# A linear-attention block beside a mixture of experts: which expert is worked first, and the column width of its plain products

## The chip, the cores and the metric

The kernel runs on one core of a Trainium2 chip. The metric is the device time of one execution in microseconds, lower is better. The engines are named as in the profile: PE (TensorE: matrix products; PEld is its load of the stationary operand), DVE (VectorE), ACT (ScalarE), POOL (GpSimd), SP (the queue from which most transfers are issued). The core has 128 partitions; PSUM, into which PE writes, has 8 banks of 512 floats per partition.

## The reference

Input is 2048 tokens of 512 numbers. The output is the input, plus a linear attention over the layer-normed tokens, plus a mixture of eight experts of which each token takes its best two:

```python
xn = layernorm(x)                                  # (2048, 512)
q, k, v = split(xn @ wqkv)                         # 32 heads of 16
phi = lambda t: where(t > 0, t + 1, exp(t)) + 1e-6
kv, z = sum_s phi(k) v^T, sum_s phi(k)             # per head
attn = (phi(q) kv) / (phi(q) z + 1e-6) @ wo
top2 = argsort(-(xn @ w_gate))[:, :2]; gates = softmax over the two logits
for e in range(8):
    h = silu(xn @ w1[e]) @ w2[e]                   # 512 -> 1792 -> 512
    out += (gates of tokens that chose e) * h
return x + attn + out
```

## The kernel before

**Precision.** Each float32 matrix is split into a high and a low part (`split_hi` on ACT, `split_lo` on DVE, lines 141 and 144), and each product is three matmuls: high x high, high x low, low x high (`PASSES`).

**Stages.** Layer norm, the key projection and the routing come first. Then a loop over token tiles computes the queries, `q_proj` (line 1376), and output products, `o_proj` (line 1437); the routing's small DVE steps run beside it. The experts fill the rest, from about 194 us on. The last output products end the program.

**Experts.** The routing ranks the eight experts by how many tokens chose them, and place r of the order works the expert of rank r with room for `CAP[r]` tokens: 576, 552, 544, 528, 520, 512, 504, 496. The tokens of an expert are gathered in blocks of 128 (`gather1`, issued on POOL). The first expert's blocks are turned by PE transposes (`x_block`, line 1093) and copied out of PSUM by ACT (line 1096). The later experts' blocks go through DRAM: `x_out` (SP, line 1109) writes 32-row groups, `x_in` (SP, line 1117) reads them back, `x_turn` (DVE, line 1126) transposes 32 x 32 blocks.

**Pairs.** An expert's 1792 hidden columns are worked as 7 pairs of 128-column tiles, so there are 56 pairs, g = 0 to 55. A pair (r, j) computes its hidden tiles, and between those products PE works pieces of the second product `mm2` of the pair before: lines 1198 and 1201. A piece is three matmuls. For an expert of at most 512 places (`single`) there are 8 pieces a pair, all 512 columns wide. A larger one has 12: two blocks of 128 tokens with 512 columns each, and four with the tokens over 256 as columns; their results are turned on DVE (`y_turn`) and added to the output in 128-column rows (`y_put`), with gate values passed round by `gate_out`, `gate_in` and `gate_up`. Three pieces of each pair are held over to the front of the next.

**Two kinds of pair.** From the third pair on, `pair_fast` computes a pair by seven products of half the tokens (`PRODUCTS`), on sums and differences of token halves and weight quarters: 7 x 2 x 3 = 42 matmuls of `CAP[r] / 2` columns (line 1316). Its results are built up in two PSUM tiles, px and pz; the tile px gets product 0, 2, 4 and then 6, and between product 4 and product 6 a DVE add (line 1343) reads it. The first two pairs (`NPLAIN`) are `pair_plain`: no sums are needed, so they can begin early; 2 hidden tiles x 2 token halves x 4 row blocks x 3 passes = 48 matmuls of 288 columns (line 1294).

**What sets the order.** Each engine runs its instructions in the order of the program, and the jobs between the products are placed by tables: `plan` puts weight splits, `x_hi`/`x_lo` (splits of the token halves B11, B12, B21, B22 and of their differences T1 to T4) and the steps of the next expert (`FIRST`, `MOVES`, `YMOVES`) behind a given product of a given pair. `places` computes addresses for `y_put` through a small transfer, at g = 2 and 4. The weights stream through a few staging buffers (`fetch_w`, lines 933 to 939, issued on SP).

Of the kernel before, what the change touches and what calls it, by code (L numbers as in the profile page):

```python
# [13 lines left out]
AF = mybir.ActivationFunctionType  # L14
ALU = mybir.AluOpType
# [5 lines left out]
P = 128  # L21
S = 2048
D = 512
KC = D // P
NT = S // P
E = 8
# [5 lines left out]
DH = 16  # L32
EPS = 1e-5

CAP = (576, 552, 544, 528, 520, 512, 504, 496)
NCOL = sum(c > 4 * 128 for c in CAP)
UW = 2 * CAP[0]
SW = 2 * D
RB = 5
OV0 = RB * E  # L40
# [45 lines left out]
def linear_attn_plus_moe(  # L86
# [11 lines left out]
    V, A, G, T, Q = nc.vector, nc.scalar, nc.gpsimd, nc.tensor, nc.sync  # L98
    x = x.rearrange("b s d -> (b s) d")
# [20 lines left out]
    def um(name):  # L120
        return wp.tile([P, UW], F32R, tag="u", name=name, bufs=20)

# [12 lines left out]
    def psm(tag, name, n=512):  # L135
        bufs = {"acc": 4, "mm": 2, "tr": 2}[tag]
        t = ps.tile([P, 512], F32, tag=tag, name=name, bufs=bufs)
        return t[:, :n]
# [63 lines left out]
    i_row = cst.tile([P, E, E], F32, name="i_row")  # L202
# [23 lines left out]
    def constants_b():  # L226
        def iota(t, pattern, base=0, cm=0):
            G.iota(t, pattern=pattern, base=base, channel_multiplier=cm,
                   allow_small_or_imprecise_dtypes=True)

        G.memset(eps6, 1e-6)
        G.tensor_copy(ones_r, ones_b)
        G.affine_select(out=tri_b, in_=ones_b, pattern=[[1, P]], compare_op=ALU.is_ge,
                        fill=0.0, base=-1, channel_multiplier=-1)
        G.affine_select(out=bmask, in_=ones.rearrange("p (a b) -> p a b", a=8),
                        pattern=[[-DH, 8], [0, DH]], compare_op=ALU.is_ge,
                        fill=0.0, base=0, channel_multiplier=1)
        G.affine_select(out=bmask, in_=bmask, pattern=[[DH, 8], [0, DH]],
                        compare_op=ALU.is_ge, fill=0.0, base=DH - 1, channel_multiplier=-1)
        iota(i_lane, [[1, P]])  # L240
        iota(i_blk, [[1, NB]])
        iota(i_ov, [[1, NOV]])
        iota(i_e8, [[0, NT], [1, E]], base=-E)
        iota(i_tok, [[P, NT]], base=1, cm=1)
        iota(i_row, [[1, E], [0, E]])
        iota(i_col, [[0, E], [1, E]])
        iota(i_tie, [[-1, E]], base=E - 1)
        iota(i_dummy[:, :OV0], [[0, E], [P, RB]], base=S + 1, cm=1)
        iota(i_dummy[:, OV0:], [[0, NOV]], base=S + 1, cm=1)
        for r in range(E):  # L250
            G.memset(i_cap[:, r:r + 1], float(CAP[r]))
        G.memset(gate, 0.0)
        for a in range(4):
            G.memset(part[a * BLK:(a + 1) * BLK], float(a))
        G.affine_select(out=lower, in_=ones[:, :E * E].rearrange("p (a b) -> p a b", a=E),
                        pattern=[[1, E], [-1, E]], compare_op=ALU.is_gt, fill=0.0, base=0,
                        channel_multiplier=0)
# [198 lines left out]
    def routing():  # L456
# [148 lines left out]
        Q.dma_start(of_d, oe)  # L605

        base = f("base", [P, E])
        V.tensor_scalar(base, rank, float(RB * P), None, op0=ALU.mult)
        d2 = f("d2", [P, E])
        V.tensor_scalar(d2, ost, float(P), float(OV0 * P), op0=ALU.mult, op1=ALU.add)  # L610
        V.tensor_tensor(d2, d2, cap, op=ALU.subtract)
# [51 lines left out]
    def table_end():  # L663
        tab = wp.tile([P, 2, NB], F32, tag="tab", name="tab", bufs=1)
        t1, em = tab[:, 0, :], tab[:, 1, :]
        V.tensor_copy(t1, tabp[0])
        V.tensor_scalar(gidx, t1, -1.0, 0.0, op0=ALU.add, op1=ALU.max)
        V.scalar_tensor_tensor(em, t1, 0.0, i_dummy, op0=ALU.is_equal, op1=ALU.mult)
        V.scalar_tensor_tensor(sidx, t1, -1.0, em, op0=ALU.add, op1=ALU.add)
        Q.dma_start(gi_d, gidx[:, OV0:])  # L670
        Q.dma_start(si_d, sidx[:, OV0:])
        t3, e3 = (a[:, :NCOL * RB].rearrange("p (r i) -> p r i", i=RB)[:, :, 2:] for a in (t1, em))
        V.scalar_tensor_tensor(s_of[:, :3 * NCOL].rearrange("p (r i) -> p r i", i=3), t3, -1.0, e3,
                               op0=ALU.add, op1=ALU.add)

# [352 lines left out]
    def half(r):  # L1028
        return CAP[r] // 2

# [6 lines left out]

    xg = {}
    XF = {}
    XR = {}  # L1040

    def gather1(r, i):
# [7 lines left out]

    def form(r, name):
        w = 2 * half(r)
        t = um(f"x{name}_{r}")
        XF[r, name] = [t[:, h * w:(h + 1) * w].rearrange("p (k c) -> p k c", k=2) for h in range(2)]

# [96 lines left out]
    def h_split(r, n, hs):  # L1152
        split(*hh[r, n], hs)
# [18 lines left out]
    def scatter(r, rows, idx, src):  # L1172
        G.memset(spacer, 0.0)  # L1173
        st = G.indirect_dma_start(out=rows, out_offset=IOA(ap=idx, axis=0), in_=src, in_offset=None,  # L1174
                                  compute_op=ALU.add).ins
        for s_ in scat[r]:
            tc.declare_no_dep(st, s_, reason="an expert's places hold different rows")
        for s_ in scat.get(r - 1, ()):
            tc.add_manual_dep(st, s_.name, mybir.DependencyInfo(
                mybir.DependencyClass.Sync, mybir.DependencyReason.DATA),  # L1180
                reason="rows of the expert before")
        scat[r].append(st)
# [94 lines left out]
    def y_put(r, k):  # L1277
        y = yu.pop((r, k))
        for c in range(y.shape[1]):
            scatter(r, out.rearrange("s (a f) -> (s a) f", a=4), sidx4[:, c, 3 * r + k:3 * r + k + 1], y[:, c])  # L1280

    def pair_plain(r, j, fill, jobs, held):
        n = half(r)
        w = W1[r, j]
        hss = h_tiles(r, j)
        for c in range(2):
            hs = hss[c]
            for q in range(2):
                fill(2 * c + q)
                hp = psm(("acc", "mm")[j], f"hp{r}_{j}_{c}{q}", n)  # L1290
                for kc in range(KC):
                    x = XF[r, f"B{kc // 2 + 1}{q + 1}"]
                    for i, (a, b) in enumerate(PASSES):
                        T.matmul(hp, w[a][:, kc, c * P:(c + 1) * P], x[b][:, kc % 2, :],
                                 start=(kc == 0 and i == 0), stop=(kc == KC - 1 and i == 2))
                A.activation(hs[:, q * n:(q + 1) * n], hp, AF.Silu)
                if q:
                    h_split(r, 2 * j + c, hs)
                jobs(2 * (2 * c + q))
                if 2 * c + q < 3:  # L1300
                    jobs(2 * (2 * c + q) + 1)
        return lambda k: None
# [277 lines left out]
    q_proj(t + 1, False)  # L1580
    x_block(0, 3)
    x_block(0, 4)
    for name in ("B11", "B21", "B12", "B22"):
        x_hi(0, name)
        x_lo(0, name)
    q_exp(t + 1)
# [8 lines left out]
    def plan(g):  # L1595
# [5 lines left out]
        def on(k, f, *args):  # L1601
            at[k].append(lambda: f(*args))
# [45 lines left out]
                on(k, (gate_out, gate_in, gate_up, y_gate, y_turn, y_put)["oiumtp".index(f)], r + e, *a)  # L1648
        if g == 0:
            on(1, x_sums, 0)  # L1650
        if g in (2, 4):
            on(6, places, g // 2 - 1)
        if j == 3 and r in (E // 2, E - 1):
            on(0, G.drain)
        if r == E - 1:
# [124 lines left out]
```

## Time and profile before

| | us |
|---|---|
| median of 3 runs | 826.53 |
| lowest and highest | 826.5, 826.88 |
| the profiled execution | 826.48 |
| its span, first to last instruction | 824.8 |
| PE busy | 820.3 (99%) |
| DVE, ACT, POOL busy | 679.6, 541.2, 249.7 |

PE is busy nearly all of the span, at a granted clock of full speed throughout. Matmuls overlap, so a matmul's own duration is longer than the distance to the next; the distance from start to start is what a matmul costs, and it is read from the timeline. A row of the timeline can stand for several instructions of the same kind (x4): its first number is the start of the first, its second the time from that start to the end of the last. Where a DVE instruction waits for a port after its start, its duration contains the wait.

### The profile page before, as it was taken

To read this page: it belongs to the slowest core of one execution; us is meant where nothing else is said; L and a number is where in the kernel's file an instruction comes from. 1 tells how busy PE (TensorE), PEld (TensorE's weight loads), DVE (VectorE), ACT (ScalarE), POOL (GpSimd) and SP (SyncE) were. 2 spreads that over 40 slices of the span, in tenths; PEclk is the share of its full clock that TensorE was granted. 3 is DMA by queue.
4 is the path that set the end of the run, shared out by engine and by line. 5 is a ranking of instruction groups with operands and counts; after the bars stand their busy time and mean duration, and the time that the engine had idled before them with its cause. 6 is when DMAs were issued, how large, how long until landed. Compare 5 with 4: busy or idle time off the path is not lost. (4 is left out here: it accounts for less than half of the span.)

```text
span 824.8 us, 15897 instructions
## 1 busy us (share of the span) xinstructions
PE 820.3 (99%) x5361; PEld 752.1 (91%) x5361; DVE 679.6 (82%) x1470; ACT 541.2 (66%) x1162; POOL 249.7 (30%) x335
## 2 busy tenths in 40 slices
PE   9999999999999999999999999999999999999998
PEld 8999888889999999999999999999999888888886
DVE  7788889999878887878888788789888987887851
ACT  5575364358666768766876777677768766776650
POOL 5543224375310136121803250443127030012002
PEclk9999999999999999999999999999999999999999
DMA  5752136354764565566557464756576573249507
GB/s 168 252 199 87 52 135 202 128 183 166 234 200 135 152 197 108 145 166 184 131 136 187 151 143 136 206 130 161 155 190 130 161 188 113 84 132 232 154 1 178
DMA packets 106874, 127.69 MB, mean 155 GB/s; under 512 B 15198, under 2 KB 69854, under 8 KB 106758
## 3 DMA queue, kind: packets, MB, share of 16 engines
q1 hardware_dynamic: 92902, 106.43, 42.7%
q0 software_dynamic: 12880, 18.66, 11.8%
q10 hardware_dynamic: 1008, 1.57, 0.5%
q8 instruction: 43, 0.70, 0.3%
q14 instruction: 41, 0.34, 0.1%
HBM read 93.95 MB, written 31.09 MB: 152 GB/s over the span
## 5 line engine op out<-in xcount | busy, mean ns | idle before, releaser
L1174 POOL DMA_INDIRECT out_dram<-yo,sidx x22 | 35.1, 1595 | 282.6 <-DVE yo L1169 260.4
L1174 POOL DMA_INDIRECT out_dram<-yu,L x47 | 78.0, 1659 | 85.9 <-ACT yu L1267 59.0
L144 DVE TENSOR_TENSOR h<-hs,h 128x576 fp32r<-128x576 f32 (+7 forms) x112 | 77.7, 694 | 5.7 <-ACT h L141 5.4
L141 ACT ACTIVATE h<-hs 128x576 fp32r<-128x576 f32 (+7 forms) x112 | 72.3, 646 | 3.2
L1324 ACT ACTIVATE hs<-px 128x276 f32<-128x276 f32 (+7 forms) x54 | 21.1, 390 | 58.7 <-PE px L1316 58.6
L1339 ACT ACTIVATE hs<-hs 128x276 f32<-128x276 f32 (+7 forms) x54 | 23.0, 426 | 46.5 <-DVE hs L1338 46.5
L1338 DVE TENSOR_TENSOR hs<-pz,hs 128x276 f32<-128x276 f32 (+7 forms) x54 | 23.3, 431 | 34.6 <-PE pz L1316 34.0
L1343 DVE TENSOR_TENSOR hs<-px,hs 128x276 f32<-128x276 f32 (+7 forms) x54 | 23.3, 432 | 33.7 <-PE px L1316 33.7
L1047 POOL DMA_INDIRECT xg<-xn_d,gidx x37 | 40.8, 1104 | 28.2 <-DMA xq<-xs_d 7.2
L437 PE MATMUL gacc<-pkhl,xnhl 128*128 128x512 f32 x192 | 47.9, 397 | 0.0
L437 PEld LDWEIGHTS gacc<-pkhl,xnhl 128*128 128x128 f32 x192 | 34.8, 188 | 6.8
L1173 POOL MEMSET spacer<- 1x1 f32 x69 | 38.4, 557 | 6.8 <-DVE ws_3l L144 6.8
L1349 DVE TENSOR_TENSOR hs<-py,hs 128x276 f32<-128x276 f32 (+7 forms) x54 | 23.0, 426 | 13.7 <-PE py L1316 13.4
L1344 ACT ACTIVATE hs<-hs 128x276 f32<-128x276 f32 (+7 forms) x54 | 22.8, 422 | 17.0 <-DVE hs L1343 15.8
L411 POOL TENSOR_TENSOR zz<-zz,pk 128x512 f32<-128x512 f32 x14 | 18.2, 1300 | 48.3 <-DVE L L404 48.3
L1385 ACT ACTIVATE e_q<-qp 128x512 f32<-128x512 f32 x16 | 9.6, 598 | 35.4 <-PE qp L1376 31.7
L1198 PE MATMUL y<-w_1h,h 128*128 128x512 f32 (+2 forms) x88 | 32.0, 394 | 0.0
L1198 PE MATMUL y<-w_5h,h 128*128 128x512 f32 (+2 forms) x88 | 32.0, 394 | 0.0
L1198 PE MATMUL y<-w_2h,h 128*128 128x512 f32 (+2 forms) x88 | 32.0, 393 | 0.0
L1198 PE MATMUL y<-w_3h,h 128*128 128x512 f32 (+2 forms) x88 | 32.0, 393 | 0.0
L1198 PE MATMUL y<-w_0h,h 128*128 128x512 f32 (+2 forms) x88 | 32.0, 393 | 0.0
L1198 PE MATMUL y<-w_4h,h 128*128 128x512 f32 (+2 forms) x88 | 31.7, 393 | 0.0
(563 smaller groups left out, 3152.8 us busy)
## 6 DMA issues: line engine op xcount, KB each, us to landing
wst<-in_B_w_dram SPq DMA_DIRECT2D x196, 128.0 KB
wst<-in_B_w_dram SPq DMA_DIRECT2D x37, 512.0 KB
zz<-in_B_w_dram SPq DMA_DIRECT2D x26, 512.0 KB
xs_d<-xg SPq DMA_DIRECT2D x117, 64.0 KB
xq<-xs_d SPq DMA_DIRECT2D x28, 256.0 KB
x<-in_A_x_dram SPq DMA_DIRECT2D x27, 256.0 KB
xn_d<-xn SPq DMA_DIRECT2D x16, 256.0 KB
xnT<-xn SPq DMA_DIRECT2D x11, 256.0 KB
```

What stands on the lines that cost most here:

```text
L141: A.activation(hi, src, AF.Copy)
L144: V.tensor_tensor(lo, src, raw(hi), op=ALU.subtract)
L437: T.matmul(gacc[d], xnhl[:, a, d * P:(d + 1) * P], pkhl[:, b, :], start=(t == 0 and i == 0), stop=(t == NT - 1 and i == 2))
L1047: G.indirect_dma_start(out=raw(t), out_offset=None, in_=xn_d, in_offset=IOA(ap=gidx[:, b:b + 1], axis=0))
L1173: G.memset(spacer, 0.0)
L1174: st = G.indirect_dma_start(out=rows, out_offset=IOA(ap=idx, axis=0), in_=src, in_offset=None, compute_op=ALU.add).ins
L1198: T.matmul(ya[r, d][:m], h[a][:, d * P:d * P + m], w[b][:, n % 2, :], start=(first and i == 0), stop=(last and i == 2))
L1338: V.tensor_tensor(c12, pz_, c12, op=ALU.add)
L1339: A.activation(c12, c12, AF.Silu)
L1343: V.tensor_tensor(c22, px, c22, op=ALU.add)
L1344: A.activation(c22, c22, AF.Silu)
L1349: V.tensor_tensor(c11, pz_, c11, op=ALU.add)
```

## The change

Place 0 of the order now works the expert of rank 5 (counted from 0; 512 places), and places 1 to 5 those of rank 0 to 4; the last two stay. The table `RANKS` says which rank a place works, and the routing, its constants and `places` follow it. With 512 places the first expert is `single`: four token blocks, no `y_turn`. Its plain pairs take all 512 columns at once, into one whole bank; the two halves of the tokens stand beside each other in a tile for the high parts and one for the low (`XP`), one pair of tiles for input rows 0 to 255, one for 256 to 511.

```diff
-CAP = (576, 552, 544, 528, 520, 512, 504, 496)
+RANKS = (5, 0, 1, 2, 3, 4, 6, 7)
+CAP = (512, 576, 552, 544, 528, 520, 504, 496)
-UW = 2 * CAP[0]
+UW = 2 * max(CAP)
...
-        iota(i_row, [[1, E], [0, E]])
+        iota(i_row, [[1, E], [0, E]], base=-1)
+        for r in (0, 6, 7):
+            G.memset(i_row[:, r, :], float(RANKS[r]))
...
-            G.memset(i_cap[:, r:r + 1], float(CAP[r]))
+            G.memset(i_cap[:, RANKS[r]:RANKS[r] + 1], float(CAP[r]))
...
-        V.tensor_scalar(base, rank, float(RB * P), None, op0=ALU.mult)
+        V.tensor_scalar(base, rank, float(RANKS[0]), None, op0=ALU.is_lt)
+        V.tensor_tensor(base, base, rank, op=ALU.add)
+        V.scalar_tensor_tensor(base, rank, float(RANKS[0]), base, op0=ALU.not_equal, op1=ALU.mult)
+        V.tensor_scalar(base, base, float(RB * P), None, op0=ALU.mult)
...
+        if r == 0 and name[0] == "B":
+            k, c = int(name[1]), int(name[2]) - 1
+            if k not in XP:
+                XP[k] = [um(f"xP{k}{h}")[:, :2 * w].rearrange("p (k c) -> p k c", k=2) for h in "hl"]
+            XF[r, name] = [t[:, :, c * half(r):(c + 1) * half(r)] for t in XP[k]]
+            return
...
         for c in range(2):
-            hs = hss[c]
+            hp = psm(("acc", "mm")[j], f"hp{r}_{j}_{c}", CAP[r])
             for q in range(2):
                 fill(2 * c + q)
-                hp = psm(("acc", "mm")[j], f"hp{r}_{j}_{c}{q}", n)
-                for kc in range(KC):
-                    x = XF[r, f"B{kc // 2 + 1}{q + 1}"]
+                x = XP[q + 1]
+                for kc in range(2):
                     for i, (a, b) in enumerate(PASSES):
-                        T.matmul(hp, w[a][:, kc, c * P:(c + 1) * P], x[b][:, kc % 2, :],
-                                 start=(kc == 0 and i == 0), stop=(kc == KC - 1 and i == 2))
-                A.activation(hs[:, q * n:(q + 1) * n], hp, AF.Silu)
+                        T.matmul(hp, w[a][:, 2 * q + kc, c * P:(c + 1) * P], x[b][:, kc, :],
+                                 start=(q == 0 and kc == 0 and i == 0), stop=(q == 1 and kc == 1 and i == 2))
                 if q:
-                    h_split(r, 2 * j + c, hs)
+                    A.activation(hss[c], hp, AF.Silu)
+                    h_split(r, 2 * j + c, hss[c])
...
-    for name in ("B11", "B21", "B12", "B22"):
+    for name in ("B11", "B12", "B21", "B22"):
         x_hi(0, name)
         x_lo(0, name)
...
-        if g in (2, 4):
-            on(6, places, g // 2 - 1)
+        if g in (9, 11):
+            on(6, places, g // 2 - 4)
```

Line numbers behind the edits grow by 1 to 13 in the changed kernel. On DVE, at the begin of the experts, the program before has these rows; `i_row` is a gate value of a token block, `xB` the low part of a token half, `den` and `pq` belong to the last query tiles:

```order
L1393 SCALAR_TENSOR_TENSOR pq_2467<-qp_2430,e_q_2443 128x512
L1077 TENSOR_TENSOR i_row<-xg_3_2387,ohr 128x8
L1077 TENSOR_TENSOR i_row<-xg_4_2410,ohr 128x8
L144 TENSOR_TENSOR xB_0_2500<-xr_0_2345,xB_0_2500 128x576
L144 TENSOR_TENSOR xB_0_2503<-xr_1_2346,xB_0_2503 128x576
L144 TENSOR_TENSOR xB_0_2506<-xr_0_2345,xB_0_2506 128x576
L144 TENSOR_TENSOR xB_0_2509<-xr_1_2346,xB_0_2509 128x576
L1410 TENSOR_REDUCE den_2516<-pz_2469 128x32
```

In the changed kernel the same place on DVE reads:

```order
L1404 SCALAR_TENSOR_TENSOR pq_2471<-qp_2434,e_q_2447 128x512
L1090 TENSOR_TENSOR i_row<-xg_3_2393,ohr 128x8
L145 TENSOR_TENSOR xP1l<-xr_0_2351,xP1h 128x2x256 x2
L145 TENSOR_TENSOR xP2l<-xr_1_2352,xP2h 128x2x256 x2
L1421 TENSOR_REDUCE den_2512<-pz_2473 128x32
```

The fifth block's gate value is gone, and the four low parts now go in pairs into two tiles, 512 columns each instead of 576. PE, first plain pair before (the two-digit names are a hidden tile and a token half):

```order
L1437 MATMUL op_0_2526<-M1h,pqT_2365 128x512
L1294 MATMUL hp_0_00_2544<-xB_0_2500,w_0_0h 128x288 x2
L1294 MATMUL hp_0_00_2544<-xB_0_2500,w_0_0l 128x288
L1294 MATMUL hp_0_00_2544<-xB_0_2500,w_0_0h 128x288 x2
L1294 MATMUL hp_0_00_2544<-xB_0_2500,w_0_0l 128x288
L1294 MATMUL hp_0_00_2544<-xB_0_2503,w_0_0h 128x288 x2
L1294 MATMUL hp_0_00_2544<-xB_0_2503,w_0_0l 128x288
```

and in the changed kernel:

```order
L1448 MATMUL op_0_2522<-M1h,pqT_2371 128x512
L1305 MATMUL hp_0_0_2540<-xP1h,w_0_0h 128x512
L1305 MATMUL hp_0_0_2540<-xP1l,w_0_0h 128x512
L1305 MATMUL hp_0_0_2540<-xP1h,w_0_0l 128x512
L1305 MATMUL hp_0_0_2540<-xP1h,w_0_0h 128x512
L1305 MATMUL hp_0_0_2540<-xP1l,w_0_0h 128x512
L1305 MATMUL hp_0_0_2540<-xP1h,w_0_0l 128x512
```

Half as many matmuls, each 512 wide, and the second of them reads the tile `xP1l`, which takes two of DVE's low parts. On DVE in the third pair (g = 2), between two splits of the weights `wa_3`, the changed kernel has

```order
L145 TENSOR_TENSOR wa_3l<-wst_2430,wa_3h 128x512
L1139 STREAM_TRANSPOSE xr_0_2775<-xq_0_2651 128x4x2x32
L1139 STREAM_TRANSPOSE xr_1_2776<-xq_0_2651 128x4x2x32
L1354 TENSOR_TENSOR hs_2_2706<-px_2_2716,hs_2_2706 128x256
L145 TENSOR_TENSOR wa_3l<-wst_2430,wa_3h 128x256
```

This order is the one of before (there with 288 columns, line 1343): the next expert's first `x_turn`, on the tile xq that `x_in` brought, and behind it the add that reads px. On SP the changed kernel no longer has the first expert's `gate_out` ahead of the first `x_out`, nor `places` among the `x_in`.

## Rows read from the trace of the kernel before

**Rows 1.** The page: busy time, share of the span and instructions of each engine, and the granted clock in 40 slices (9 is full speed).

```profile
PE 820.3 (99%) x5361; PEld 752.1 (91%) x5361; DVE 679.6 (82%) x1470; ACT 541.2 (66%) x1162; POOL 249.7 (30%) x335
...
PEclk9999999999999999999999999999999999999999
```

**Rows 2.** Two stretches at the begin of the experts: from:to, length, busy us (and instructions) of PE, PEld, DVE, ACT, POOL, granted clock, DMA share, GB/s.

```profile
194.00:215.00 21.00, 21.00 (x148) 20.48 (x148) 20.73 (x37) 15.09 (x29) 10.53 (x11) 1.00 0.38 107
215.00:235.00 20.00, 20.00 (x135) 19.20 (x134) 15.49 (x35) 12.32 (x27) 5.54 (x8) 1.00 0.94 307
```

**Rows 3.** Timeline of PE, 190 to 222 us: start us, us, engine, line, operation, out<-in, shape, count. The first two rows bound eight transposes, the next two the 48 matmuls of the first plain pair; at 211.03 the pieces held over from the second pair begin, at 212.86 the third pair's product 0 (six matmuls), at 222.10 its product 6.

```profile
190.34 0.80 PE L1093 MATMUL xep<-ident_r,xg 128*128 128x128 f32 x8
190.97 0.46 PE L1437 MATMUL op<-M0h,pqT 128*128 128x512 f32 x1
...
193.79 0.43 PE L1294 MATMUL hp<-xB,w_0h 128*128 128x288 f32 x2
...
200.18 0.43 PE L1294 MATMUL hp<-xB,w_1h 128*128 128x288 f32 x2
...
211.03 0.46 PE L1201 MATMUL y<-h,w_0h 128*128 128x320 f32 x2
...
212.86 0.42 PE L1316 MATMUL px<-xB,wa_2h 128*128 128x288 f32 x2
...
213.66 0.45 PE L1201 MATMUL y<-h,w_1h 128*128 128x320 f32 x2
...
222.10 0.43 PE L1316 MATMUL px<-xT,wa_2h 128*128 128x288 f32 x2
```

**Rows 4.** Timeline of PE in the expert of 512 places, where the products are 256 wide: six matmuls of one product between the first row and the second, nine matmuls of 512 columns between the third and the fourth.

```profile
596.44 0.40 PE L1316 MATMUL pz<-xB,ws_1h 128*128 128x256 f32 x2
...
597.15 0.40 PE L1198 MATMUL y<-w_0h,h 128*128 128x512 f32 x1
...
601.37 0.40 PE L1198 MATMUL y<-w_0h,h 128*128 128x512 f32 x1
...
603.44 0.40 PE L1316 MATMUL px<-xB,wa_2h 128*128 128x256 f32 x2
```

**Rows 5.** Timeline of ACT and of POOL around the begin of the experts; in brackets the idle time ahead and what ended it.

```profile
191.69 2.43 ACT L141 ACTIVATE xB<-xr 128x576 fp32r<-128x576 f32 x4
...
191.84 1.30 POOL L1397 TENSOR_TENSOR pz<-pq,zz 128x512 f32<-128x512 f32 x1
...
207.72 1.31 POOL L1416 TENSOR_TENSOR pz<-pq,den 128x512 f32<-128x512 f32 x1 [4.89 <-DVE den L1415]
```

**Rows 6.** Timeline of DVE, 192 to 212 us.

```profile
192.43 3.34 DVE L144 TENSOR_TENSOR xB<-xr,xB 128x576 fp32r<-128x576 f32 x4 [0.45 <-ACT xB L141]
...
198.82 1.75 DVE L1132 TENSOR_TENSOR xr<-xr,xr 128x576 f32<-128x576 f32 x1
...
202.72 0.20 DVE L1250 STREAM_TRANSPOSE gt<-gate 128x32 f32<-128x32 f32 x1
202.85 0.38 DVE L988 TENSOR_TENSOR wr<-wst 128x256 f32<-128x256 f32 x1
...
203.61 0.75 DVE L144 TENSOR_TENSOR xT<-xr,xT 128x576 fp32r<-128x576 f32 x1
204.28 0.75 DVE L144 TENSOR_TENSOR h<-hs,h 128x576 fp32r<-128x576 f32 x1
...
206.29 0.68 DVE L1410 TENSOR_REDUCE den<-pz 128x32 f32<-128x512 f32 x1
...
210.24 0.68 DVE L144 TENSOR_TENSOR ws_2l<-wr,ws_2h 128x512 fp32r<-128x512 f32 x1
210.84 0.70 DVE L144 TENSOR_TENSOR wa_2l<-wst,wa_2h 128x512 fp32r<-128x512 f32 x1
```

**Rows 7.** Timeline of SP's queue: the last query tile's `pz_out`, the first eight transfers of `x_out`, the first `x_in`, the next weights.

```profile
209.05 0.33 SPq L1441 DMA_DIRECT2D pz_d<-pz  x1
209.47 3.77 SPq L1109 DMA_DIRECT2D xs_d<-xg  x8
213.71 0.34 SPq L1117 DMA_DIRECT2D xq<-xs_d  x1
214.28 0.41 SPq L939 DMA_DIRECT2D wst<-in_B_w_dram  x1
```

**Rows 8.** Timeline of DVE in the third pair: the first `x_turn` and the add that reads px.

```profile
219.92 0.77 DVE L1126 STREAM_TRANSPOSE xr<-xq 128x256 f32<-128x256 f32 x2 [0.79 <-DMA xq<-xs_d]
220.61 0.42 DVE L1343 TENSOR_TENSOR hs<-px,hs 128x288 f32<-128x288 f32 x1
```

**Rows 9.** Timeline of ACT and of DVE behind that: the second product's weights of the third pair (w_2), and the high and the low part of that pair's first hidden tile.

```profile
221.27 0.63 ACT L141 ACTIVATE w_2h<-wst 128x512 fp32r<-128x512 f32 x1 [1.95 <-DMA wst<-in_B_w_dram]
...
223.12 0.69 ACT L141 ACTIVATE h<-hs 128x576 fp32r<-128x576 f32 x1
...
223.84 0.76 DVE L144 TENSOR_TENSOR h<-hs,h 128x576 fp32r<-128x576 f32 x1 [0.25 <-ACT h L141]
224.52 0.69 DVE L144 TENSOR_TENSOR w_2l<-wst,w_2h 128x512 fp32r<-128x512 f32 x1
```

**Rows 10.** Timeline of DVE in the routing, at the step that the change replaces by four.

```profile
136.82 0.17 DVE L610 TENSOR_SCALAR arena<-arena 128x8 f32<-128x8 f32 x1
137.02 0.17 DVE L611 TENSOR_TENSOR arena<-arena 128x8 f32<-128x8 f32 x1
```

More of the change, by code (lines that the diff above doesn't have):

```diff
@@ L671, in table_end @@
         Q.dma_start(si_d, sidx[:, OV0:])
-        t3, e3 = (a[:, :NCOL * RB].rearrange("p (r i) -> p r i", i=RB)[:, :, 2:] for a in (t1, em))
+        t3, e3 = (a[:, RB:(NCOL + 1) * RB].rearrange("p (r i) -> p r i", i=RB)[:, :, 2:] for a in (t1, em))
         V.scalar_tensor_tensor(s_of[:, :3 * NCOL].rearrange("p (r i) -> p r i", i=3), t3, -1.0, e3,
@@ L1039, in linear_attn_plus_moe @@
     XF = {}
+    XP = {}
     XR = {}
@@ L1279, in y_put @@
         for c in range(y.shape[1]):
-            scatter(r, out.rearrange("s (a f) -> (s a) f", a=4), sidx4[:, c, 3 * r + k:3 * r + k + 1], y[:, c])
+            scatter(r, out.rearrange("s (a f) -> (s a) f", a=4), sidx4[:, c, 3 * r + k - 3:3 * r + k - 2], y[:, c])
     def pair_plain(r, j, fill, jobs, held):
-        n = half(r)
         w = W1[r, j]
```

## Prediction

> **What bounds the kernel now.** I read the busy times first. PE is busy 820.3 us of a span of 824.8 us, with the granted clock at its upper level in all 40 slices [rows 1], and through both stretches in which the change lies it is busy every microsecond of them [rows 2]. So the time is a sum of matmuls. An edit pays only by what it takes from that sum, and it costs whatever new gap it opens on PE. Next I read the timeline of PE for the price of each kind of matmul, by the distance from start to start, since the durations overlap [rows 3, 4]. Last come the engines behind the new matmuls: DVE is full from 194 to 215 us (20.73 of 21.00 us), and from 215 to 235 us it is the DMA engines (share 0.94) [rows 2]. A PE that runs faster here runs towards both. The profiled execution took 826.48 us, 0.05 less than the median of 826.53; the sum is made against it.
>
> **PE's sum.** *Plain products.* The 48 matmuls of the first pair run from 193.79 to 200.18 us, 6.39/48 = 0.133 us each [rows 3]; two pairs have 96, 12.78 us. After the change they are 48 of 512 columns. Nine such took 601.37 to 603.44 us, 0.230 each, so 0.231 with rounding [rows 4]: 11.09 us. That is **-1.69**.
>
> *Fast products.* The expert of 512 places had seven fast pairs and now has five; the one of 576 goes from five to seven. So 2 x 42 = 84 matmuls go from 256 to 288 columns. Six of 256 took 596.44 to 597.15 us, 0.1183 each [rows 4]; six of 288 took 212.86 to 213.66 us, 0.1333 each [rows 3]. 84 x 0.015 = **+1.26**. This eats three quarters of the gain: the total of hidden columns is the same, and only the start-up share of each matmul is saved.
>
> *Transposes.* The fifth block of the first expert goes, four of the eight transposes between 190.34 and 190.97 us [rows 3]: 0.63/2 = **-0.31**. The second products (pieces) of every expert stay the same, only their place in the program changes. Sum for PE: -1.69 + 1.26 - 0.31 = **-0.74**.
>
> **Small things off PE.** Three more steps of 128x8 in the routing follow one another in 0.20 us each (136.82 to 137.02 us) [rows 10]. PE has its query products beside them, so I take 0; without that cover they would cost 0.6. Three POOL fills stand at the program's begin, and POOL is busy 30% [rows 1]: 0. `gate_out`, its transpose on DVE (0.13 us, 202.72 to 202.85) [rows 6] and the move of `places` to a later pair only free queues. The fifth block of the expert of 520 places now goes through DRAM, one more `x_in` and two more turns on DVE (0.69 for two, 219.92 to 220.61) [rows 8] deep inside an expert: 0, or at most their 0.69.
>
> **First new wait: the low parts.** PE reaches its first plain matmul at 193.79 - 0.31 = 193.48 us and its second 0.23 later, at 193.71. The second reads the tile `xP1l`, whose two low parts are the first two of DVE's four. Before, the four took from 192.43 to 195.69 us, 3.34 us together [rows 6], where such an operation's pitch is 0.67 (203.61 to 204.28); three at 0.67 leave 3.34 - 2 x 0.67 - 0.75 = 1.25 for the first. The excess fits POOL, which runs an operation from 191.84 to 193.14 us [rows 5]; the first low part seems to get going only behind it. At 512 columns the pitch is 0.60 (210.24 to 210.84). So the first ends at 193.14 + 0.56 = 193.70 us, the second at 194.30, and PE waits 194.30 - 193.71 = **+0.6**. If ACT, which makes two evictions fewer ahead of its high parts (from 191.69) [rows 5], lets DVE in before POOL, it is 0; if the first operation takes as long as before and all hand-overs are slow, 0.9. I take 0.6, since both the begin of POOL's operation and the pitch are read from rows.
>
> The Trainium skill ("SBUF — State Buffer", section "SBUF: two separate sides") says that DVE and GpSimd share a port pair under an exclusive lock, and that the loser waits. The trace agrees: beside POOL's work the operation at 198.82 us lasts 1.75 us against 0.75 [rows 6]. By the rule the first wait stays; without it, it would be 0 and the sum 0.6 lower.
>
> **Second new wait: the add on px.** In the third pair, product 6 rebuilds px, so it must stand behind the DVE add of line 1343 (before). DVE works in order, and ahead of this add stands the first `x_turn` of the next expert, which waits for `x_in` to land. Before, DVE sat idle 0.79 us for that landing, turned from 219.92 us, and the add ended at 220.61 + 0.42 = 221.03 [rows 8]; PE came to product 6 at 222.10 [rows 3], 1.07 later. That slack was all of the cover.
>
> After, PE comes sooner. First pair: 193.48 + 0.6 + 24 x 0.231 = 199.62. Second pair: 24 x 0.231 + 5 pieces of 3 x 0.231 = 9.01, to 208.63 (211.03 before). Three held pieces: 2.08, to 210.71 (212.86 before). Then six products of 0.71 and five pieces of 0.693, 7.73: product 6 is due at **218.44**, 3.66 earlier. The reason for so much is that the gain in the plain pairs comes at once, narrow pieces move behind, and the wider fast pairs that pay for it come later.
>
> The landing does not come so much sooner. It hangs on a chain: DVE's `den` at 206.29 us [rows 6], POOL at 207.72 [rows 5], SP's `pz_out` at 209.05, eight `x_out` from 209.47, `x_in` at 213.71 [rows 7], landing at 219.92 [rows 8]. DVE is full up to `den`, so it is earlier by what DVE saves: 0.06 and 3 x 0.07 on the low parts, 4 x 0.07 on the sums of line 1132, 4 x 0.07 on splits of 576, 0.13 for the transpose, together 0.96; I take 0.93. Then the landing is at 218.99, and the add ends at 218.99 + 0.69 + 0.42 = 220.10. PE waits 220.10 - 218.44 = **+1.66**. From below: if the transfers land 1.66 sooner still, 0. From above: if they land as before, since the DMA engines are full from 215 us on, 221.03 - 218.44 = 2.6. I take 1.66, as each link of the chain stands directly behind the one before.
>
> Behind that, the third pair's first hidden tile is needed at 220.10 + 0.71 + 3 held pieces (2.08) + 2 products (1.42) = 224.31 us. Before, its low part was done at 224.52 [rows 9], through a chain from the landing of w_2 at 221.27. Those weights are issued on SP right behind the `x_in` (214.28) [rows 7], so they also move by 0.93, and the tile is ready at 223.59: no wait. From there on the slack on PE's side is spent, and the pairs have the pace of the other experts of this kind, in which PE is fully busy.
>
> **Sum:** -0.74 + 0.6 + 1.66 = +1.5, so 826.48 + 1.5 = **828.0 us**.
>
> **Rivals.** A run can tell about 0.2% from no change, 1.65 us: under 824.88 is faster, over 828.18 slower.
>
> *A, as summed* (0.52): 828.0. Its own spread, from the two hand-overs and DVE's share of the chain, is about half a microsecond to either side, and some 0.21 of the 0.52 lie over 828.18.
>
> *B, the second wait does not come* (0.25): the `x_in` has 6.2 us from issue to landing, much of it in a crowd of `x_out`, gathers and weights [rows 2, 7]. A transfer that meets less of the crowd, since it starts earlier, lands in time for 217.33 us. Then -0.74 + 0.6 gives 826.3; but PE would then need the first hidden tile at 222.65, 0.94 before it is ready, which gives 827.3. Between the two: 826.8. For it speaks the low DMA share of the stretch before (0.38), against it that the crowd is issued by the same chain. If the first wait goes too, 825.7.
>
> *C, slower* (0.18): the DMA engines decide. If the landings do not move at all, the sum is -0.74 + 0.6 + 2.6 = +2.5, or 829.0; if earlier weight requests push `x_in` back by half a microsecond, 829.5. It decides from a landing later than 219.2 us. For it speaks the share of 0.94, against it that the chain's links before the DMA engines do move.
>
> *D, the row price does not hold for the plain products* (0.05): in a bank of their own the 512-wide matmuls could run with no start-up at all, 512/2.4 = 0.213 us from the granted clock's upper level (2.4 GHz), 48 x 0.018 = 0.9 less, and neither wait might matter: 824.9 at best. Of this 0.03 is put under 824.88.
>
> The Trainium skill ("TensorE: Matmul & The Clock Gate", section "Back-to-back issue gap") gives some 131 ns for a sustained matmul of 512 columns. By that, as an estimate, the plain stage would be 48 x 0.131 = 6.3 us and the kernel near 823. The trace speaks against it with 0.230 [rows 4]; its chance is within the 0.03.
>
> **Numbers.** Likeliest is A, 828.0. For 8 in 10 the range takes in A, most of C and B without its lower end: 826.0 to 829.5. Faster: 0.03. Slower: C's 0.18 and 0.21 of A, 0.39. Within 0.2%: the rest of A and nearly all of B, 0.58.
>
> **What would show it.** Right: 48 matmuls at 0.231 us in the plain pairs and fast pairs of 0.71 and 0.80 per product at the new places; a gap on PE near 0.6 us behind the very first plain matmul; DVE idle for `x_in` longer than 0.79 us ahead of the first turn, and a gap on PE near 1.7 us ahead of product 6 of the third pair; PE's gaps unchanged elsewhere. Wrong: no gap at product 6 (B); a gap over 2.5 us there, or one ahead of the first piece that reads w_2 (C); a different pitch at 512 columns (D). A gap at the passage from the first expert to the second, whose gather and turns are now for 576 places, would be one that I have not costed.

## The result, and the profile after

The changed kernel takes **831.26 us** in the median (830.13 to 832.65), against 826.88 us for the kernel before beside it (826.5 to 827.12): a ratio of 1.0053, with a 95% interval of 1.004 to 1.0066. It is 0.5% slower, some 4.4 us. The forecast was 828.0 us in a range of 826.0 to 829.5. The profiled execution took 830.33 us, its span is 828.6 us; 3.8 us over the span of before.

The page still shows a PE that is busy 99%, with 52 matmuls fewer (as in [rows 1]):

```profile
PE 819.9 (99%) x5309; PEld 748.2 (90%) x5309; DVE 679.8 (82%) x1474; ACT 540.2 (65%) x1156; POOL 249.6 (30%) x339
```

So the loss is not in this line, since its busy time has fallen by 0.4 us, and the granted clock is again at full speed in all 40 slices. It is in a few gaps. The timeline of PE shows them where the idle time ahead of a row is in brackets; a wait that ends in the first hundreds of nanoseconds is partly hidden by the overlap of matmuls, so the gap is the distance from the row before to this one, less what the matmul before costs without a wait (answers to [rows 3]):

```profile
140.81 0.39 PE L1387 MATMUL qp<-wq1h,xnT 128*128 128x512 f32 x1
141.64 0.66 PE L1433 MATMUL pqp<-ident_r,pz 128*128 128x128 f32 x4 [0.44 <-POOL pz L1427]
...
194.21 0.39 PE L1305 MATMUL hp<-xP1h,w_0h 128*128 128x512 f32 x1
195.09 0.50 PE L1305 MATMUL hp<-xP1l,w_0h 128*128 128x512 f32 x1 [0.49 <-DVE xP1l L145]
...
200.44 0.39 PE L1305 MATMUL hp<-xP1h,w_1h 128*128 128x512 f32 x1
...
211.32 0.28 PE L1327 MATMUL px<-xP1h,wa_2h 128*128 128x256 f32 x1
...
216.03 0.39 PE L1211 MATMUL y<-w_1h,h 128*128 128x512 f32 x1
216.50 0.50 PE L1327 MATMUL px<-xT,ws_2h 128*128 128x256 f32 x2
...
219.19 0.39 PE L1211 MATMUL y<-w_1h,h 128*128 128x512 f32 x1
221.43 0.50 PE L1327 MATMUL px<-xT,wa_2h 128*128 128x256 f32 x2 [1.85 <-DVE hs L1354]
```

A matmul of 512 columns costs 0.23 us here, so the four gaps are 0.60 us at 140.8 us (in the query stage, 50 us ahead of the experts), 0.65 at the first plain matmul, 0.24 ahead of product 4 and 2.01 ahead of product 6 of the third pair. Another 0.84 us lies behind the last matmul: from its start to the end of the span it is 4.15 us, and 3.31 before.

DVE shows what the first gap comes from. The one step of [rows 10] is now four, each dependent on the one before:

```profile
136.74 0.17 DVE L611 TENSOR_SCALAR arena<-arena 128x8 f32<-128x8 f32 x1
136.94 0.17 DVE L612 TENSOR_TENSOR arena<-arena 128x8 f32<-128x8 f32 x1
137.14 0.17 DVE L613 SCALAR_TENSOR_TENSOR arena<-arena 128x8 f32<-128x8 f32 x1
137.35 0.17 DVE L614 TENSOR_SCALAR arena<-arena 128x8 f32<-128x8 f32 x1
...
139.10 0.68 DVE L1421 TENSOR_REDUCE den<-pz 128x32 f32<-128x512 f32 x1
...
140.52 1.06 POOL L1427 TENSOR_TENSOR pz<-pq,den 128x512 f32<-128x512 f32 x1 [4.96 <-DVE den L1426]
```

In the kernel before, the same `den`, POOL's `pz` behind it and PE's turn of `pz` stand here:

```profile
138.49 0.68 DVE L1410 TENSOR_REDUCE den<-pz 128x32 f32<-128x512 f32 x1
139.92 1.06 POOL L1416 TENSOR_TENSOR pz<-pq,den 128x512 f32<-128x512 f32 x1 [4.35 <-DVE den L1415]
141.03 0.66 PE L1422 MATMUL pqp<-ident_r,pz 128*128 128x128 f32 x4
```

There is no idle time on DVE between the four steps and `den`, so all three come 0.6 us late. The next rows are an operation of POOL and, beside it, the two low parts of the first plain matmuls on DVE, 2.28 us for both (the next two take 1.28). Then comes the third pair, in which DVE waits longer for the landing of `x_in` than before, 2.46 us against 0.79, and the landing is later, not earlier ([rows 8], there 219.92):

```profile
192.58 1.31 POOL L1408 TENSOR_TENSOR pz<-pq,zz 128x512 f32<-128x512 f32 x1
192.76 2.28 DVE L145 TENSOR_TENSOR xP1l<-xr,xP1h 128x512 fp32r<-128x512 f32 x2
194.97 1.28 DVE L145 TENSOR_TENSOR xP2l<-xr,xP2h 128x512 fp32r<-128x512 f32 x2
...
220.30 0.77 DVE L1139 STREAM_TRANSPOSE xr<-xq 128x256 f32<-128x256 f32 x2 [2.46 <-DMA xq<-xs_d]
220.99 0.39 DVE L1354 TENSOR_TENSOR hs<-px,hs 128x256 f32<-128x256 f32 x1
```

though its request on SP came 0.11 us earlier than in [rows 7]:

```profile
208.88 0.32 SPq L1452 DMA_DIRECT2D pz_d<-pz  x1
209.29 3.83 SPq L1122 DMA_DIRECT2D xs_d<-xg  x8
213.60 0.34 SPq L1130 DMA_DIRECT2D xq<-xs_d  x1
```

Without the gaps, PE's matmuls can be summed by kind over the two traces: the plain products went from 12.79 to 11.01 us (-1.78), the fast products of 256 and 288 columns together rose by 1.43, the transposes fell by 0.29: -0.64, where the forecast had -0.74.

### The profile page after: what moved, and what is told of

It is laid out like the page before. It is cut to its first block, busy times and chain, and to the rows that moved or that the text cites. A ratio compares the mean times of both kernels' runs of the same rounds, so it can differ in the third digit from the quotient of the medians.

```text
span 828.6 us, 15793 instructions
## 1 busy us (share of the span) xinstructions
PE 819.9 (99%) x5309; PEld 748.2 (90%) x5309; DVE 679.8 (82%) x1474; ACT 540.2 (65%) x1156; POOL 249.6 (30%) x339
## 4 chain that ended last, share of the span: by engine, by line
PE 88%; DVE 6%; DMA 3%; POOL 1%; issue 1%; SPq 1%; ACT 0%; ACTq 0%; another core or an unknown queue 0%; POOLq 0%; DVEq 0%
PE y L1211 24%; PE px L1327 19%; PE y L1214 13%; PE pz L1327 9%; PE k L387 5%; PE gacc L440 5%; PE py L1327 5%; PE qp L1387 4%; PE op L1448 2%; DMA xq<-xs_d 1%; DMA xo<-out_dram 1%; DMA out_dram<-yo,sidx 1%; POOL out_dram L1187 1%; DMA wkst<-in_A_wqkv_dram 1%; DVE den L1421 1%
## 5 line engine op out<-in xcount | busy, mean ns | idle before, releaser
L145 DVE TENSOR_TENSOR h<-hs,h 128x512 fp32r<-128x512 f32 (+7 forms) x112 | 77.5, 692 | 5.6 <-ACT h L142 5.1
L142 ACT ACTIVATE h<-hs 128x512 fp32r<-128x512 f32 (+7 forms) x112 | 72.3, 646 | 3.2
L1335 ACT ACTIVATE hs<-px 128x288 f32<-128x288 f32 (+7 forms) x54 | 21.1, 391 | 53.3 <-PE px L1327 49.9
L1350 ACT ACTIVATE hs<-hs 128x288 f32<-128x288 f32 (+7 forms) x54 | 23.0, 427 | 46.4 <-DVE hs L1349 44.6
L1354 DVE TENSOR_TENSOR hs<-px,hs 128x288 f32<-128x288 f32 (+7 forms) x54 | 23.4, 433 | 34.8 <-PE px L1327 34.8
L1349 DVE TENSOR_TENSOR hs<-pz,hs 128x288 f32<-128x288 f32 (+7 forms) x54 | 23.3, 431 | 32.6 <-PE pz L1327 30.1
L1355 ACT ACTIVATE hs<-hs 128x288 f32<-128x288 f32 (+7 forms) x54 | 22.8, 422 | 18.9 <-DVE hs L1354 18.0
L1360 DVE TENSOR_TENSOR hs<-py,hs 128x288 f32<-128x288 f32 (+7 forms) x54 | 23.0, 425 | 13.5 <-PE py L1327 12.7
L1345 ACT ACTIVATE hs<-px 128x288 f32<-128x288 f32 (+7 forms) x54 | 21.2, 392 | 16.7 <-PE px L1327 14.3
```

Source lines behind the costliest of these rows:

```text
L142: A.activation(hi, src, AF.Copy)
L145: V.tensor_tensor(lo, src, raw(hi), op=ALU.subtract)
L1354: V.tensor_tensor(c22, px, c22, op=ALU.add)
```

## The experiments

The theory after the result (A): the change costs by gaps in a chain. The added routing steps take 0.6 us from a DVE without slack; PE then gets ahead of `x_in`, whose request hangs on the chain `den`, norm, `pz_out`, `x_out`, and product 6 waits since its add stands behind an `x_turn` on DVE. The main rival (B): the DMA engines set the landing whatever the request does. Medians of runs on several chips are compared through the kernel before beside them (826.7 to 827.0 us); the last two experiments are single executions. The changed kernel itself was executed six times ahead of the experiments and once in experiment 11, with 829.49 us, which is under the lowest of the six (830.13). So a difference of about a microsecond from its median of 831.26 shows nothing by itself, and the readings below rest on the gaps in the traces.

**1. Routing steps on POOL.**

```diff
...
+        G.tensor_scalar(low, rank, float(RANKS[0]), None, op0=ALU.is_lt)
+        G.tensor_tensor(low, low, rank, op=ALU.add)
+        G.tensor_scalar(base, rank, float(RANKS[0]), -float(RB * P), op0=ALU.is_equal, op1=ALU.mult)
+        G.tensor_scalar(base, base, float(RB * P), None, op0=ALU.add)
+        G.tensor_tensor(base, base, low, op=ALU.mult)
         yield 2.6
...
-        V.tensor_scalar(base, rank, float(RANKS[0]), None, op0=ALU.is_lt)
-        V.tensor_tensor(base, base, rank, op=ALU.add)
-        V.scalar_tensor_tensor(base, rank, float(RANKS[0]), base, op0=ALU.not_equal, op1=ALU.mult)
-        V.tensor_scalar(base, base, float(RB * P), None, op0=ALU.mult)
```

> The changed kernel, with the four routing steps that make the expert's place from its rank moved from DVE to POOL (five small operations there, issued one stretch earlier). Theory A (the waits add along a chain: the three added steps hold DVE for 0.6 us, so POOL's pz and PE's turn at 140.8 us come 0.6 late, and everything behind, x_in too): PE's gap of 0.6 us at 140.8 us goes, x_in lands 0.6 earlier, PE's gap ahead of product 6 of the third pair stays near 2.0 us, the time falls by 0.6 us. Theory B (the DMA engines set the landing, whenever the request comes): the gap at 140.8 goes, x_in lands at the same time, the gap ahead of product 6 grows to 2.6 us and the time doesn't fall.

832.36 us (831.25 to 833.65), ratio 1.0069. The gap at 140.8 us is gone, the gap ahead of product 6 is 3.03 us:

```profile
218.86 0.39 PE L1213 MATMUL y<-w_1h,h 128*128 128x512 f32 x1
222.12 0.50 PE L1329 MATMUL px<-xT,wa_2h 128*128 128x256 f32 x2 [2.87 <-DVE hs L1356]
```

PE's saving went into the wait, as B has it for this run. But most of the earlier request that A counts on got lost on the way. This execution stands 0.55 us later at the `kvp` matmuls near 110 us, ahead of the routing steps; counted from there, `den` came 0.81 us sooner than in the changed kernel (205.85 us against 206.11), and `x_in` only 0.24 (213.91 against 213.60). Between them POOL's `pz` began 0.45 us behind DVE's last step in place of 0.15 and took 1.61 us in place of 1.32; why isn't shown. A new gap of 0.66 us stands at 294 us. Landings of the same request order differ by over a microsecond between executions (below), so this run alone doesn't decide between A and B.

**2. The last `pz_out` one pair later on SP.**

```diff
             q_norm(NT - 1)
+        if g == 1:
             pz_out(NT - 1)
```

> The changed kernel, with SP's last pz_out put one pair later, behind the first eight x_out, the first x_in and the weights, so that these no longer wait for the last query tile's den and norm. Theory A (the landing hangs on the chain den, norm, pz_out, x_out): the x_out start near 206 us in place of 209.3, x_in lands near 217 in place of 220.3, PE's gap of 2.0 us ahead of product 6 goes, and the time falls by 2 us, perhaps a few tenths less since the next need (the third pair's w_2 weights) comes closer. Theory B (the DMA engines set the landing): x_in lands less than 1 us earlier, more than 1 us of the gap stays, the time falls by less than 1 us.

829.24 us (828.49 to 830.3), ratio 1.0031 (1.002 to 1.0042): 2.0 us below the median of the changed kernel (1.0053, 1.004 to 1.0066). The `x_out` and the `x_in` go out 5 us earlier, DVE no longer waits for the landing, and the gap at product 6 is gone:

```profile
204.15 3.82 SPq L1122 DMA_DIRECT2D xs_d<-xg  x8
208.21 0.90 SPq L1130 DMA_DIRECT2D xq<-xs_d  x1
```

```profile
217.72 0.77 DVE L1139 STREAM_TRANSPOSE xr<-xq 128x256 f32<-128x256 f32 x2
```

So the place of the request decides, if it moves by microseconds, out of the stretch in which the DMA engines are full (share 0.08 from 205 to 210 us in the changed kernel, 0.91 from 210 to 220). Gaps of 0.39 and 0.17 us came near 291 us.

**3. Low parts by rows.**

```diff
     for name in ("B11", "B12", "B21", "B22"):
-        x_hi(0, name)
-        x_lo(0, name)
+        form(0, name)
+    for q in range(2):
+        for k in range(2):
+            hi, lo = (t[:, k, :] for t in XP[q + 1])
+            split_hi(hi, XR[0, q][:, k, :CAP[0]])
+            split_lo(hi, lo, XR[0, q][:, k, :CAP[0]])
```

> The changed kernel, with the first expert's high and low parts made by input rows (128 rows, all 512 columns in one operation) and no longer by token halves, so that the second plain matmul needs one low part and not two. Theory A (only the last wait counts, and product 6 hangs on x_in, which doesn't depend on PE): the gap of 0.66 us behind the first plain matmul falls under 0.15, PE comes 0.55 sooner to product 6 and waits 2.5 there: the time stays within 0.2 us. Rival (the waits add): the time falls by 0.55 us.

830.31 us (828.93 to 833.4), ratio 1.005. The gap of 0.65 us is gone; in its place come one of 0.20 at 210.5 us (on `wa_2l`), 0.31 ahead of product 4 and 1.61 ahead of product 6, where this execution's landing was 0.84 us sooner, at 219.46 us (near 110 us it is already 0.29 ahead of the changed kernel's). The two low parts took 2.27 us as before, so the gap came of the second plain matmul's need for both. The median is 0.95 us lower, within the spread of both, so neither forecast (the same within 0.2, or 0.55 less) is shown.

**4. The order alone, plain products in halves** (the matmuls, the tiles and the order of the low parts as before, 256 columns).

> The changed kernel with its order of experts, but with the plain products of the first expert over token halves as in the kernel before (96 matmuls of 256 columns). Theory A (the order costs, by the routing steps and by x_in coming too late for a PE that gets through the first pairs sooner): the first gap falls to 0.2 us or less, the plain products cost 0.27 us more, PE waits about 2.2 us ahead of product 6, the time is that of the changed kernel within 0.3 us. Rival (the 512-column products cost): the gap ahead of product 6 falls under 1 us and the time by over 1 us.

830.21 us (829.65 to 834.4), ratio 1.0053. The first gap is 0.18 us, the one ahead of product 6 is 0.90 with a landing at 219.7 us, and 0.67 us are lost at 293 us. The ratio, with one execution of 834.4 us in it, is that of the changed kernel, but the median is 1.05 us lower and the gap ahead of product 6 is under 1 us, which was the sign of the rival. The second profile of the changed kernel (experiment 11) has 0.79 us there as well, so the gap is no mark of the 512 columns. That most of the loss comes with the order is shown by a kernel that is still 0.4 to 0.5% slower without them; what the 512 columns cost by their two gaps (0.65 and 0.24 us, here 0.18 and none) isn't settled by the time.

**5. Three more steps in the kernel before.**

```diff
-        V.tensor_scalar(base, rank, float(RB * P), None, op0=ALU.mult)
+        V.tensor_scalar(base, rank, 2.0, None, op0=ALU.mult)
+        V.tensor_scalar(base, base, 5.0, None, op0=ALU.mult)
+        V.tensor_scalar(base, base, 8.0, None, op0=ALU.mult)
+        V.tensor_scalar(base, base, float(RB * P) / 80.0, None, op0=ALU.mult)
```

> The kernel before, with its one routing step (the expert's base from its rank) written as four dependent steps of the same shape, the result the same. Theory A (the three added steps hold a DVE that has no slack there): a gap of 0.6 us on PE at 140.8 us as in the changed kernel, and the time rises by 0.6 us, since in this kernel everything behind moves along with it, x_in too. Rival (the steps lie beside PE's work, as the prediction had it): no gap, no change.

827.39 us (827.03 to 827.74) against 826.98: +0.4 us, ratio 1.0004 (0.9995 to 1.0013). The gap on PE is there in full, 0.67 us, in a kernel with nothing else changed:

```profile
141.50 0.66 PE L1425 MATMUL pqp<-ident_r,pz 128*128 128x128 f32 x4 [0.50 <-POOL pz L1419]
```

The time's interval holds both 0 and 0.6; the trace shows the mechanism.

**6. Edits 1 to 3 together.**

> The changed kernel with three edits together: the routing steps on POOL, the low parts by input rows, the last pz_out behind the first x_out and x_in. Theory A (the gaps of 0.6, 0.66 and 2.0 us are the cost of the change, and the early request gives x_in enough lead): all three go, x_in lands near 217 us, PE's sum of -0.74 remains, with a gap of some 0.3 us ahead of product 4 and some 0.5 us near 290 us as in the runs so far: 3.0 to 3.5 us below the changed kernel, 827.5 to 828. Rival (PE that is 1.2 us sooner meets x_in or the weights w_2 again): a gap of 0.5 us or more ahead of product 6 or of the first piece on w_2, and the time is 828.5 or more.

828.28 us (826.55 to 829.36), ratio 1.001 (1.0001 to 1.0019), between the two forecasts. All three gaps are gone, and the profiled execution, the slowest of the eleven, shows the same mechanism one pair later: an add on DVE behind an `x_turn` that waits 3.68 us, and PE behind the add.

```profile
231.75 0.77 DVE L1141 STREAM_TRANSPOSE xr<-xq 128x256 f32<-128x256 f32 x2 [3.68 <-DMA xq<-xs_d]
232.44 0.39 DVE L1362 TENSOR_TENSOR hs<-py,hs 128x256 f32<-128x256 f32 x1
```

```profile
231.77 0.39 PE L1213 MATMUL y<-w_2h,h 128*128 128x512 f32 x1
232.98 0.36 PE L1329 MATMUL px<-xP1h,wa_4h 128*128 128x256 f32 x1 [0.82 <-DVE hs L1362]
```

**7. The first `x_turn` behind the add.**

```diff
-         5: ((1, "i", 1), (2, "o", 2), (3, "o", 3), (3, "t", 0), (4, "o", 4), (5, "i", 2), (6, "i", 3)),
+         5: ((1, "i", 1), (2, "o", 2), (3, "o", 3), (4, "o", 4), (5, "t", 0), (5, "i", 2), (6, "i", 3)),
```

> The changed kernel, with the next expert's first x_turn moved on DVE from between product 3 and 4 of the third pair to behind product 5, so that it stands behind the add that reads px. The landing of x_in isn't touched. Theory A (product 6 waits only since the add stands behind an x_turn that waits): the gap of 2.0 us ahead of product 6 goes; PE then comes 2 us sooner to the first piece on w_2, whose hidden tile hangs on weights that land at 221.7 us, and waits there 1.4 us: the time falls by 0.6 us. Rival (product 6 waits for something else, such as PSUM or ACT): the gap stays over 1 us and the time is unchanged.

830.13 us (828.89 to 831.28), ratio 1.0044. The add runs at 217.6 us, the gap at product 6 is gone with an untouched request, and 1.30 us stand instead between products 0 and 1 of the next pair. There PE needs a PSUM tile that ACT empties, and ACT stood 3.46 us for the weights w_2 (in [rows 9] 1.95):

```profile
221.34 0.63 ACT L142 ACTIVATE w_2h<-wst 128x512 fp32r<-128x512 f32 x1 [3.46 <-DMA wst<-in_B_w_dram]
```

```profile
222.68 0.28 PE L1327 MATMUL px<-xP1h,wa_3l 128*128 128x256 f32 x1
224.10 0.50 PE L1327 MATMUL pz<-xT,ws_3h 128*128 128x256 f32 x2 [1.15 <-ACT hs L1367]
```

This shows the order on DVE as the cause of the 2.0 us, and the next landing right behind it.

**8. The late `pz_out` in the kernel before.**

> The kernel before, with only the last pz_out moved one pair later as in the run on the changed kernel. Theory A (the early request pays by the gap that it closes, and this kernel has none there): no change, within 0.2 us, though x_in lands some 3 us earlier. Rival (the move pays or costs by itself, by the DMA engines being spread better or worse): a change of 0.5 us or more, with the same sign as in the changed kernel.

826.79 us (826.32 to 827.44) against 826.98, ratio 0.9999 (0.999 to 1.0008): nothing, as there was no gap to close. So the gain of experiment 2 is that of the closed gap, and no gift of the move itself.

**9 and 10. All edits, and only the two on the passage.** The fourth edit moves the turns of the first passage behind the adds (those of blocks 0, 2 and 4; block 3 stays where it was); run 10 has it with the late `pz_out`, without the edits to routing and low parts.

```diff
-         5: ((1, "i", 1), (2, "o", 2), (3, "o", 3), (3, "t", 0), (4, "o", 4), (5, "i", 2), (6, "i", 3)),
-         4: ((0, "i", 4), (0, "f"), (1, "t", 1), (4, "t", 2)),
-         3: ((0, "t", 3), (2, "t", 4), (5, "s"))}
+         5: ((1, "i", 1), (2, "o", 2), (3, "o", 3), (4, "o", 4), (5, "i", 2), (6, "t", 0), (6, "i", 3)),
+         4: ((0, "i", 4), (0, "f"), (1, "t", 1), (6, "t", 2)),
+         3: ((0, "t", 3), (3, "t", 4), (5, "s"))}
```

> The run with three edits (steps on POOL, low parts by rows, pz_out late) and a fourth: the first expert's passage to the second keeps no x_turn ahead of an add on DVE; the turns of blocks 0 and 2 stand at the ends of the third and fourth pair, those of blocks 3 and 4 one product later. Theory A (what PE still waits for in the run with three edits, 0.98 and 0.50 us near 232 us, is again an add behind a turn that waits for its landing, one pair later): both gaps go, PE's sum of -0.74 is left with 0.2 to 0.5 us of small gaps: 826.5 to 827.2, level with the kernel before. Rival (the DMA engines are full, so some need waits whatever the order): a new gap of over 0.5 us between 215 and 250 us, 827.8 or more.

> The changed kernel with only the two edits on the passage: pz_out late and the turns behind the adds. Theory A (the costs of the routing steps, 0.6 us, and of the low parts, 0.66 us, are paid in full once PE no longer waits for x_in): 1.2 us above the run with four edits, 827.8 to 828.4. Rival (these two gaps only take the place of waits further on): level with the run with four edits, within 0.4 us.

828.54 us (827.76 to 829.5), ratio 1.0022 (1.0013 to 1.0032), and 829.0 us (828.11 to 829.79), ratio 1.0027 (1.0017 to 1.0036). In both, PE has no gap over 0.3 us between 200 and 285 us. But run 9 isn't level with the kernel before: 0.42 and 0.14 us are lost near 290 us (0.65 in run 10), 0.27 ahead of product 4, 0.44 more than before ahead of an output product near 814 us, and 0.36 behind the last matmul. Against the kernel before beside it, run 9 is 1.84 us slower and run 6 was 1.30: the fourth edit closed the gap near 232 us and no gain in time shows. Run 10 is only 0.46 us slower than run 9, though it has 1.35 us more in the two early gaps. So these don't add in full even with the passage free; 0.44 of the difference is the gap near 814 us, which run 10's profile lacks, and where the rest is made up isn't shown.

**11 and 12. Second profiles.**

> The changed kernel once more, for a second profile. Theory A: gaps of 0.6, 0.66, 0.24 us at 141, 194 and 216 us to within 0.1, since they come of the order of instructions; the gap ahead of product 6 may differ by half a microsecond with the landing of x_in; a gap near 290 us, as in four of the runs, may or may not come.

> The kernel before once more, for a second profile: no gap over 0.15 us on PE between 110 and 810 us, and 3.3 us from the last matmul's start to the end of the span, to within 0.2; over 3.6 us would say that the changed kernel's 4.1 is no mark of the change.

829.49 and 826.95 us. The changed kernel repeats its gaps with 0.67, 0.68 and 0.23 us. The one ahead of product 6 is 0.79 here, 2.01 in the first profile, with a landing 1 us sooner for a request 0.38 us later (213.98 us), more than the half microsecond allowed for:

```profile
219.31 0.77 DVE L1139 STREAM_TRANSPOSE xr<-xq 128x256 f32<-128x256 f32 x2 [1.24 <-DMA xq<-xs_d]
```

It has 0.45 and 0.14 us near 291 us, which the first profile lacks. The kernel before has none of these, and 3.29 us behind its last matmul. Such a spread of landings would fit that the changed kernel's six executions vary by 2.5 us and those of the kernel before beside them by 0.6; it isn't shown, and the kernel before varies by 1.5 and 2.0 us over the 27 and 18 executions beside the later experiments.

## Why the prediction was wrong

*PE's sum* was right: -0.74 forecast, -0.64 measured. A 512-column matmul cost 0.229 us (0.231 forecast), so rival D falls. The 131 ns that the Trainium skill gives for a sustained matmul of 512 columns ("TensorE: Matmul & The Clock Gate", section "Back-to-back issue gap") does not hold for this stream.

*The first wait* was right in place and size, 0.65 us for 0.6, and run 3 shows that it came of the two low parts. That POOL is what makes the first of them long fits the rows (2.28 us for two beside POOL's operation, 1.28 for the next two), but no run takes POOL away.

*The step that failed first* is in "Small things off PE": "PE has its query products beside them, so I take 0; without that cover they would cost 0.6". The cover was looked for on PE, which is the wrong engine. The steps stand on DVE ahead of `den`, DVE has no idle time there, and PE waits for `den` through POOL one tile later. The cost was the 0.6 us named as the price without cover; runs 1 and 5 show the gap by taking it away and by making it alone, though neither settles 0.6 us in the time. By itself this would have left the forecast at 828.6 us, inside the range; the miss is the sum of this and of what follows.

*The second wait* was right as a mechanism, shown by runs 2 and 7; its size was off: 2.01 and 0.79 us in two profiles, 1.66 forecast. The term was mis-sized at "I take 0.93" for how much sooner `x_in` lands. Its request was only 0.11 us sooner, as the 0.6 us of the routing had set DVE back; run 1 shows that this wasn't all, since there, without these steps, `den` came 0.81 us sooner and the request only 0.24, the rest being lost at POOL. The landing was 0.38 us later than before in the one profile and 0.6 sooner in the other. Both are later than 219.2 us, the sign that the prediction gave for rival C; the cause that C named, the DMA engines, is only part of it, since the request itself hardly moved. The slack behind it (224.31 against 223.59) held: with the wait in place no gap follows. In run 7, without it, PE waits 1.30 us for what hangs on w_2, where rival B had 0.94.

*What the sum left out:* the gap of 0.24 us ahead of product 4, where ACT's copy of px out of PSUM (its eviction) stands behind a weight split that itself waits for DVE:

```profile
215.55 0.63 ACT L142 ACTIVATE ws_3h<-wr 128x512 fp32r<-128x512 f32 x1 [1.00 <-DVE wr L998]
216.09 0.37 ACT L1345 ACTIVATE hs<-px 128x256 f32<-128x256 f32 x1
```

Further, the passage to the second expert, which the prediction named as not costed, with 0.4 to 0.7 us near 290 us in seven of the ten profiles with the new order and in none of the four with the old one; and the end of the program, 0.3 to 1.15 us (0.84 in the first profile, 0.35 in the second). With the first profile's 0.60 + 0.65 + 0.24 + 2.01 + 0.84, the -0.64 and some 0.1 us in small ones, 3.8 us of the span are accounted for. The median lies 0.9 us above the profiled execution; by the spread of run 11 that is the landing and the gap near 290 us, which is argued, not shown.

*Still open:* what delays ACT near 290 us. There its eviction of px starts 1.2 to 1.9 us behind the end of the matmuls that it needs, and what the profile names as releaser differs from run to run and had been done by then. In run 1:

```profile
290.74 0.29 PE L1329 MATMUL px<-xB,wa_2l 128*128 128x288 f32 x1
292.24 0.41 ACT L1337 ACTIVATE hs<-px 128x288 f32<-128x288 f32 x1 [2.66 <-issue]
```

The DMA engines have a share of 1.06 from 280 to 290 us in the changed kernel and 0.77 before; there the first expert's output now goes out as four whole blocks. That this is the cause wasn't tried, and the share alone is not enough, as the profile with 1.06 is one without the gap. No version here beats the kernel before.

## What to carry to other kernels

Ask for the cover of an added step on the engine that runs it, not on the bound engine: a full queue passes the delay on to whoever waits behind it, here 0.6 us by way of POOL to PE. When the bound engine is made faster in one place, list every transfer whose landing was just in time there; each can be a new wait, and when one is removed the next is close behind (runs 6 and 7). A request is worth moving out of a stretch in which the DMA engines are full if the bound engine waits for it (run 2; in run 8, where it doesn't, the same move gave nothing), and a wait for a landing should not stand ahead of short work that the bound engine needs.

## What was not expected of the hardware

Two executions of one program had landings 1 us apart for the same request (6.70 and 5.33 us behind its issue) in a stretch with a DMA share of 0.91, while the gaps set by instruction order repeated to 0.1 us.

At the end of the program SP waits for the semaphores of its transfers one after another, 0.06 us each. In the changed kernel's trace the last write's semaphore is followed by five more waits, in the kernel before it is the last in the list: some 0.3 us of the longer end. That this comes of the changed number of transfers ahead is how we read the list; it wasn't tried. The rest of the first profile's 0.84 us goes with a wait of 0.92 us on DVE for the output tile `xo` at 823.14 us. The last write itself was done 2.3 to 2.4 us behind the last matmul's start in both second profiles.
